# Batch 2's scaled r and k turned by the transposing DMA, with a new stored order and a stored PSUM bank for every tile

## The chip, the cores and the metric

One Trainium2 chip, one of its cores. The metric is the device time of one execution in microseconds (us). A core has five engines with a queue each, and each works through its queue in order: TensorE (PE, matrix products), ScalarE (ACT), VectorE (DVE), GpSimd (POOL) and SyncE (SP), which here only issues DMAs. PE writes to PSUM, which this kernel uses as 8 banks of 128 x 512 fp32; everything else lies in SBUF, 128 partitions wide.

## The reference, cut to what matters

Inputs are r, k, v, w of shape [4, 8, 768, 48] (batch, head, step, channel), u [8, 48], and two weights, 384 x 1536 and 1536 x 384. A recurrence over the steps is followed by a Fourier mix and a small network:

```python
for t in range(S):                       # attention, per batch and head
    cur = outer(u * k[t], v[t])
    y[t] = r[t] @ (state + cur)
    state = w[t][:, None] * state + outer(k[t], v[t])
x = y.transpose(0, 2, 1, 3).reshape(B, S, H * D)          # [4, 768, 384]
mixed = real(fft(fft(x, axis=1), axis=2))
u = x + mixed
un = (u - mean(u)) / sqrt(var(u) + 1e-6)                   # over the 384
out = u + relu(un @ w_ch1) @ w_ch2
```

## The kernel before, in words

The kernel takes each batch in 6 chunks of 128 steps; `n` is the number of a chunk over all four batches, 0 to 23. Batch 0 takes its chunks in pairs (`attention2`), the others one by one (`attention`).

**Attention of a chunk.** ACT takes the logarithm of w. PE sums it over the steps with a triangular matrix (L933, L937), ACT takes the exponentials (L939, L952). DVE and POOL scale r (L971) and k by them; r and k lie in one tile, `rkh`, 128 steps x 2 x 8 heads x 64 in bf16 (a head's 48 channels are padded to 64). Beside that, POOL or DVE multiply r, k and the bonus u (`rk<-in_r,in_k` and `rk<-rk,ub`), DVE sums over a head (`dc`), and the product with v is `vtd`.

The products of r and k (`amat`, L1003) need them with the channels on the partitions, as tile `rkt`. There are two ways:

- For `n < DMA_T`, PE turns them: `tr_r` (L987) and `tr_k` (L993), four 128 x 128 transposes each into a PSUM bank, and then an eviction of 128 x 512 for each, by ACT (L550) or DVE (L551).
- For `n >= DMA_T`, a single transposing DMA, issued by SP (L979), does it from SBUF to SBUF:

```python
if n >= DMA_T:
    op("sp", T_RK, lambda e: e.dma_start_transpose(out=RKT[i4][:, :, :],
                       in_=RKH[i4][:, :, :, :].rearrange("t x h d -> t (x h d)")),
       r=[("RH", i4), ("KH", i4)], w=[("RTB", i4), ("KTB", i4)], sem="rkt%d" % i4, xfer=T_XFER)
```

`DMA_T` is 18: batch 3 alone goes by DMA. Then DVE masks `amat`'s result (`ah`, L1008), PE computes the state (L1029) and the result (L1050, L1053), and DVE adds `vtd` (L1059), which gives x.

**The mix of a batch.** x is folded into its even and odd parts (`xf`, and for batches from `FOLD` on by way of `sd`); PE multiplies by cosines and sines along the steps (L1117) and the channels (L1140). DVE adds x (`uf`, L1142) and takes mean and variance; ACT or DVE subtract the mean (`un`). `un` is turned by PE for batches 0 and 1 (L1163), by a transposing DMA for batches 2 and 3 (L1169).

**The network of a batch**, per half of 384 steps: 12 times three matmuls with W1 (L1187, 128 x 384), relu to `ht` by ACT (L1194) or DVE (L1192), then for each of three blocks of 128 steps 12 matmuls with W2 (L1205), which DVE scales and adds to `uf` (`osb`, L1209), and a write to the output (L1213). The very last block is made in a piece of 256 and one of 128 columns.

**Loads.** r, k, v and w of each chunk are loaded by SP (L579 in pairs, L587 one by one), each kind into 7 buffers in turn. POOL issues the loads of W1 and W2 (L745).

**The order.** Every instruction is first recorded as an operation with a number, what it reads and what it writes. The tables `ORDER["pe"]`, `["act"]`, `["dve"]`, `["pool"]` and `["sp"]` list the numbers in the order in which each engine does them; where an operation may go to more than one engine (`vec`, `evict`), the table in which it stands decides. The waits follow from what is read and written. `schedule` replays the tables against a model of durations, only to give each PSUM tile a bank: the one that is free first in that model. A tile that takes over a bank waits for all operations of the tile before it in that bank.

Of the kernel before, what the change touches and what calls it, by code (L numbers as in the profile page):

```python
# [7 lines left out]
ALU = mybir.AluOpType  # L8
# [14 lines left out]
DMA_T, DMA_U, T_RK, T_UN, T_XFER = 18, 2, 1750, 2000, 1800  # L23
# [10 lines left out]
ORDER = {  # L34
# [24 lines left out]
    "act": (  # L59
# [13 lines left out]
    "dve": (  # L73
# [15 lines left out]
    "pool": (  # L89
# [11 lines left out]
}  # L101


class _Tile:


# [1175 lines left out]
```

## Time and profile before

Three runs took 184.76, 186.2 and 187.23 us: the median is 186.2. The profiled execution:

| | |
|---|---|
| span of the profiled execution (its own time) | 185.4 us |
| PE busy | 176.7 us, 95% |
| weight loads beside it | 126.0 us, 68% |
| DVE busy | 151.6 us, 82% |
| ACT busy | 128.7 us, 69% |
| POOL busy | 106.6 us, 58% |
| DMA, mean over the span | 157 GB/s, 29.01 MB |
| chain that ended last, by engine | PE 74%, DVE 9%, ACT 7%, DMA 6% |

A slice is a fortieth of the span, 4.6 us. Busy PE is time in which matmuls are on their way, not time at its peak. In a chain of waits each row is the work that the next had to wait for; "L1187 x9" is a run of nine matmuls of that line. In a group's row the number behind the comma is the mean duration of one instruction in ns; then comes the idle time ahead of these instructions and what ended it. The names are those of the program's tiles, with the numbers of buffers left out.

### The profile page before, as it was taken

The numbers are of one execution on the slowest core, as the hardware profiler recorded it, in microseconds if no ns is written. First come the engines' busy times: TensorE is split into PE (matmuls) and PEld (weight loads), VectorE is DVE, ScalarE is ACT, GpSimd is POOL, SyncE is SP. The second block draws the span as 40 slices with busy tenths as digits, with TensorE's granted clock in tenths as the row PEclk, the third lists the DMA queues.
The fourth block names the chain that finished last, engine by engine and source line by source line (L and its number), as shares of the span: only waits on it lengthen the run. The fifth ranks groups of instructions, "written<-read, shape, count | busy, mean of one in ns | idle before, by whom it ended". The sixth has DMA issues, their size and how long they took to land.

```text
span 185.4 us, 4736 instructions
## 1 busy us (share of the span) xinstructions
PE 176.7 (95%) x1824; PEld 126.0 (68%) x1824; DVE 151.6 (82%) x360; ACT 128.7 (69%) x303; POOL 106.6 (58%) x128
## 2 busy tenths in 40 slices
PE   5999999997999999999999999999999999999993
PEld 2355676754788768767785777758788666887771
DVE  7979999999499999999999999999897297180043
ACT  5989999996799577899588789726745513627120
POOL 2359999799958826999694659868645000000000
PEclk9999999998799999999999999999999999999999
DMA  6999998999999899899498399692811005412033
GB/s 158 325 301 257 218 194 176 193 194 186 209 211 196 162 196 216 195 224 212 89 213 174 70 234 164 116 183 56 205 46 42 4 0 139 117 42 88 0 127 127
DMA packets 102600, 29.01 MB, mean 157 GB/s; under 512 B 98865, under 2 KB 102066, under 8 KB 102450
## 3 DMA queue, kind: packets, MB, share of 16 engines
q1 hardware_dynamic: 102034, 26.36, 64.8%
q0 software_dynamic: 544, 2.36, 6.7%
q8 instruction: 14, 0.23, 0.5%
q14 instruction: 8, 0.07, 0.1%
HBM read 23.59 MB, written 4.72 MB: 153 GB/s over the span
## 4 chain that ended last, share of the span: by engine, by line
PE 74%; DVE 9%; ACT 7%; DMA 6%; issue 2%; POOL 1%; POOLq 0%; DVEq 0%; ACTq 0%
PE bank L1205 24%; PE bank L1187 24%; DMA w<-in_moe_w_ch_dram 6%; PE bank L1140 5%; PE bank L1117 3%; DVE ah L856 2%; PE bank L1003 2%; PE bank L1226 2%; PE bank L1053 2%; PE bank L1248 2%; ACT rkt L550 1%; PE bank L1050 1%; ACT lb L541 1%; DVE xf L527 1%; PE bank L933 1%
## 5 line engine op out<-in xcount | busy, mean ns | idle before, releaser
L1187 PE MATMUL bank<-unt,w 128*128 128x384 bf16 x288 | 57.5, 335 | 1.0 <-DMA w<-in_moe_w_ch_dram 0.8
L1194 ACT ACTIVATE ht<-bank 128x384 bf16<-128x384 f32 x88 | 39.9, 496 | 24.4 <-PE bank L1187 24.0
L1205 PE MATMUL bank<-w,ht 128*128 128x384 bf16 (+2 forms) x300 | 53.0, 320 | 0.0
L1187 PEld LDWEIGHTS bank<-unt,w 128*128 128x128 bf16 x288 | 38.5, 145 | 8.3 <-DMA w<-in_moe_w_ch_dram 1.0
L1205 PEld LDWEIGHTS bank<-w,ht 128*128 128x128 bf16 x300 | 28.0, 98 | 15.6
L1209 DVE SCALAR_TENSOR_TENSOR osb<-bank,rstd,uf 128x384 f32<-128x384 f32 (+2 forms) x25 | 14.4, 594 | 17.8 <-PE bank L1205 13.3
L1008 DVE TENSOR_TENSOR ah<-bank,msk 128x512 bf16<-128x512 f32 x36 | 23.2, 678 | 0.9 <-PE bank L1003 0.7
L527 POOL TENSOR_TENSOR rkh<-in_k,e 128x384 bf16<-128x384 f32 x20 | 19.9, 997 | 5.6 <-ACT e L952 5.3
L527 POOL TENSOR_TENSOR rk<-rk,ub 128x384 f32<-128x384 f32 x18 | 18.6, 1038 | 5.5 <-DVE rk L527 2.4
L527 POOL TENSOR_TENSOR vtd<-in_v,dc 128x384 f32<-128x384 f32 (+1 forms) x22 | 18.1, 827 | 3.7 <-DVE dc L960 3.7
L527 POOL TENSOR_TENSOR rk<-in_r,in_k 128x384 f32<-128x384 f32 x18 | 18.2, 1020 | 0.0
L541 ACT ACTIVATE un<-uf,agg 128x384 bf16<-128x384 f32 x20 | 12.1, 615 | 7.1 <-DVE agg L1148 7.1
L550 ACT ACTIVATE rkt<-bank 128x512 bf16<-128x512 bf16 x24 | 15.1, 633 | 1.6 <-PE bank L987 1.6
L527 POOL TENSOR_TENSOR sd<-x 128x385 f32<-128x385 f32 x9 | 9.4, 1046 | 11.2 <-DVE sd L527 5.4
L1142 DVE TENSOR_TENSOR uf<-bank,x 128x384 f32<-128x384 f32 x24 | 12.9, 549 | 2.4 <-PE bank L1140 2.2
L527 POOL TENSOR_TENSOR xf<-sd 128x382 bf16<-128x382 f32 (+1 forms) x9 | 10.4, 1164 | 4.5 <-DVE sd L527 4.3
L1146 DVE BATCH_NORM_STATS2 bst<-uf 128x6 f32<-128x384 f32 x24 | 12.7, 546 | 0.1
L939 ACT ACTIVATE bank<-bank 128x384 f32<-128x384 f32 x18 | 8.8, 493 | 5.7 <-PE bank L933 5.7
L1059 DVE TENSOR_TENSOR x<-bank,vtd 128x384 f32<-128x384 f32 x18 | 9.7, 547 | 3.3 <-PE bank L1053 3.3
L541 ACT ACTIVATE lb<-in_w 128x384 bf16<-128x384 f32 (+1 forms) x21 | 12.1, 576 | 0.3 <-PE bank L798 0.2
L541 ACT ACTIVATE vb<-in_v 128x384 bf16<-128x384 f32 x22 | 11.4, 532 | 0.0
L952 ACT ACTIVATE e<-bank 128x392 f32<-128x392 f32 (+1 forms) x18 | 8.9, 497 | 2.5 <-DVE bank L1037 1.1
(167 smaller groups left out, 356.4 us busy)
## 6 DMA issues: line engine op xcount, KB each, us to landing
out_dram<-osb SPq DMA_DIRECT2D x23, 192.0 KB, 2.3
in_w<-in_w_dram SPq DMA_DIRECT2D x18, 192.0 KB, 4.3
in_k<-in_k_dram SPq DMA_DIRECT2D x18, 192.0 KB, 4.0
in_r<-in_r_dram SPq DMA_DIRECT2D x18, 192.0 KB, 3.9
in_v<-in_v_dram SPq DMA_DIRECT2D x18, 192.0 KB, 3.8
w<-in_moe_w_ch_dram POOLq DMA_DIRECT2D x2, 1152.0 KB, 10.6
in_w<-in_w_dram SPq DMA_DIRECT2D x3, 384.0 KB, 4.6
in_k<-in_k_dram SPq DMA_DIRECT2D x3, 384.0 KB, 4.6
```

Source lines behind the costliest of these rows:

```text
L527: return lambda e: e.tensor_tensor(out=o, in0=a, in1=b, op=f)
L541: return lambda e: e.activation(o, a, f, **kw)
L550: {"act": lambda e: e.activation(o(), i(), ACTF.Copy), "dve": lambda e: e.tensor_copy(out=o(), in_=i())}, **kw)
L1008: masked[n] = op("dve", v_1(512), lambda e, x=x: e.tensor_tensor(out=ah[:, x:H:2, :], in0=ps(ta[x])[:, :].rearrange("p (h t) -> p h t", t= ...
L1059: op("dve", v_1(DM), lambda e: e.tensor_tensor(out=xb[:, c, 0:DM], in0=ps(ty)[:, 0:DM], in1=vtd[:, :, :].rearrange("t h d -> t (h d)"), op ...
L1140: return e.matmul(ps(t)[:, 0:DM], (hcs if kb < NP else HCR)[:, j, a:a + 128], DTM[:, j, :], start=(j == 0), stop=(j == 2))
L1142: op("dve", v_1(DM), lambda e, kb=kb, t=t: e.tensor_tensor(out=uf[:, kb, :], in0=ps(t)[:, 0:DM], in1=xb[:, kb, 0:DM], op=ALU.add), r=[t, ( ...
L1146: op("dve", v_1(DM), lambda e, kb=kb, bs=bs: e.bn_stats(bs[:, :], uf[:, kb, :]), r=[("UF", i, kb)], w=[("BST", n % 4)])
L1187: ins = e.matmul(ps(t)[:, 0:384], W1[:, m, j:HID:NJ], unt[:, :, m, :], start=(m == 0), stop=(m == NM - 1))
L1194: "act": lambda e, j=j, t=t, ht=ht: e.activation(ht[:, j, :], ps(t)[:, 0:384], ACTF.Relu, scale=-1.0)},
L1205: ins = e.matmul(ps(t)[:, 0:hi - lo], ht[:, j, 128 * x:128 * x + 128], W2[:, j, lo:hi], start=(j == 0), stop=(j == NJ - 1))
L1209: op("dve", v_1(hi - lo) + 64, lambda e, kb=kb, t=t, o=o, lo=lo, hi=hi: e.scalar_tensor_tensor(out=o[:, lo:hi], in0=ps(t)[:, 0:hi - lo], s ...
```

## The change

`DMA_T` goes from 18 to 12, so that the six chunks of batch 2 (n = 12 to 17) take the transposing DMA too. The 12 groups of four transposes on PE and their 12 evictions go, and six transposing DMAs come onto SP. All five tables in `ORDER` are new. A second table, `BANKS`, has for each bank the tiles that use it in order; `schedule` shrinks to taking the engine from `ORDER` and the bank from `BANKS`, and the waits of an instruction are sorted by its place in the order. The model of durations is gone; the numbers that were its costs remain in the calls and change nothing in the program.

```diff
-DMA_T, DMA_U, T_RK, T_UN, T_XFER = 18, 2, 1750, 2000, 1800
+DMA_T, DMA_U, T_RK, T_UN, T_XFER = 12, 2, 1300, 1300, 1800
...
 ORDER = {
     "pe": (
-        "6 1437 1438 1439 1440 1441 1442 1443 86 92 1444 1445 1446 94 1447 1448 80 1449 1450 97 1451 1452 113 115 "
...
+        "6 1419 1420 1421 1422 1423 1424 86 1425 1426 1427 1428 1429 92 1430 1431 1432 1433 94 1434 80 82 97 1435 1436 "
...
+BANKS = (
+    "0 10 89 97 92 48 98 101 51 60 62 113 55 58 119 79 182 86 135 137 203 152 202 191 205 253 161 206 251 271 234 238 "
+    "282 287 288 302 308 315",
...
-    def schedule(self, order):
+    def schedule(self, order, banks):
         self.order = {e: [self.ops[int(i)] for i in order[e].split()] for e in self.ENGS}
...
         for e in self.ENGS:
             for o in self.order[e]:
                 o.eng = e
-                o.dur, o.fn, o.port = o.alts[e]
...
+                o.fn = o.alts[e][1]
+        for b, line in enumerate(banks):
+            last = None
+            for i in line.split():
+                t = self.tiles[int(i)]
+                t.bank = b
+                if last is not None:
+                    t.ops[0].deps |= set(last.ops)
+                last = t
...
-                for c, v, d in sorted(o.waits, key=lambda x: x[2].end):
+                for c, v, d in sorted(o.waits, key=lambda x: x[2].at):
...
-    g.schedule(ORDER)
+    g.schedule(ORDER, BANKS)
```

The instructions per engine: the changed kernel has 48 matmuls fewer on PE; DVE takes 20 of the relu evictions instead of 8, and 6 evictions of `rkt` instead of 12; ACT takes 76 relu evictions instead of 88, and 18 of `rkt` instead of 24.

Lines in the changed kernel: `tr_r` L908, `tr_k` L914, the transposing DMA of r and k L900, `amat` L924, state L950, `vec` L448, loads L508, the loads of W1 and W2 L666, cosines and sines L1038, W1 L1108, W2 L1126, `osb` L1130, writes L1134.

**SP.** The queue while batch 2's inputs are loaded, before:

```order
43 L587 DMA in_v<-in_v_dram 128x8x48 x3
44 L587 DMA in_w<-in_w_dram 128x8x48 x2
45 L587 DMA in_v<-in_v_dram 128x8x48
46 L587 DMA in_k<-in_k_dram 128x8x48
47 L587 DMA in_r<-in_r_dram 128x8x48 x2
48 L587 DMA in_w<-in_w_dram 128x8x48
49 L1213 DMA out_dram<-osb 128x384 x2
50 L587 DMA in_k<-in_k_dram 128x8x48
```

and now; `rkt<-rkh` is the transposing DMA of a chunk, the first two are those of batch 2's chunks 0 and 1:

```order
41 L508 DMA in_v<-in_v_dram 128x8x48
42 L900 DMA_TRANSPOSE rkt<-rkh 128x8x128
43 L508 DMA in_w<-in_w_dram 128x8x48
44 L900 DMA_TRANSPOSE rkt<-rkh 128x8x128
45 L508 DMA in_k<-in_k_dram 128x8x48
46 L508 DMA in_v<-in_v_dram 128x8x48
47 L508 DMA in_k<-in_k_dram 128x8x48
48 L1134 DMA out_dram<-osb 128x384 x2
49 L508 DMA in_r<-in_r_dram 128x8x48
50 L1134 DMA out_dram<-osb 128x384
51 L508 DMA in_r<-in_r_dram 128x8x48 x2
```

Between the loads of batch 2 now stand transposes, each of which waits for `rkh`.

**POOL.** Its queue up to the load of W1 (`w1<-`), from the same product of v on, before:

```order
21 L527 TENSOR_TENSOR vtd0<-in_v,dc0 128x384
22 L527 TENSOR_TENSOR rk0<-rk0,ub 128x384
23 L527 TENSOR_TENSOR rkh3<-in_k,e2_0 128x8x48
24 L531 TENSOR_SCALAR sd<-sd,th 128x128 x2
25 L527 TENSOR_TENSOR rk2<-in_r,in_k 128x384
...
37 L527 TENSOR_TENSOR xf0<-x0 128x192
38 L527 TENSOR_TENSOR xf0<-x0 128x191
39 L745 DMA w1<-in_moe_w_ch1_dram 128x3x1536
40 L527 TENSOR_TENSOR rk2<-rk2,ub 128x384
```

and now:

```order
29 L448 TENSOR_TENSOR rk1<-rk1,ub 128x384
30 L448 TENSOR_TENSOR rk2<-rk2,ub 128x384
31 L448 TENSOR_TENSOR vtd0<-in_v,dc1 128x384
32 L448 TENSOR_TENSOR xf0<-x0 128x192
33 L448 TENSOR_TENSOR rkh2<-in_k,e2_0 128x8x48
34 L448 TENSOR_TENSOR vtd1<-in_v,dc2 128x384
35 L448 TENSOR_TENSOR xf0<-x0 128x191 x2
36 L448 TENSOR_TENSOR xf0<-x0 128x192
37 L448 TENSOR_TENSOR xf0<-x0 128x191
38 L666 DMA w1<-in_moe_w_ch1_dram 128x3x1536
39 L448 TENSOR_TENSOR xf0<-x0 128x192
40 L448 TENSOR_TENSOR xf0<-x0 128x191
```

Counted over the whole queue ahead of it: before, 2 of the `sd` masks, 2 products of r and k, 3 products with the bonus and 8 folds `xf`; now no `sd` mask, 1 product of r and k, 5 with the bonus and 5 folds. Two folds moved behind it; the fills (memsets) differ by a few small ones.

**PE.** A place in batch 2 where r and k were turned, before:

```order
227 L1117 MATMUL bank<-cs,xf 128x193 x6
228 L993 MATMUL bank<-idw,rkh 128x128 x4
229 L1117 MATMUL bank<-ss,xf 128x193
230 L1117 MATMUL bank<-cs,xf 128x193
231 L1029 MATMUL bank<-vb,rkh 128x96 x4
232 L987 MATMUL bank<-idw,rkh 128x128 x4
233 L1117 MATMUL bank<-cs,xf 128x193 x3
```

and the same stage now:

```order
227 L1038 MATMUL bank<-cs,xf 128x193 x4
228 L1126 MATMUL bank<-w,ht 128x384 x4
229 L924 MATMUL bank<-rkt 128x128 x8
230 L1038 MATMUL bank<-cs,xf 128x193 x4
231 L1038 MATMUL bank<-ss,xf 128x193 x2
```

The transposes (L993, L987) are gone; `amat` (L924) waits for the DMA. At the program's end, PE's last rows before:

```order
519 L1205 MATMUL bank<-w,ht 128x384 x12
520 L1205 MATMUL bank<-w,ht 128x256 x8
521 L1205 MATMUL bank<-w,ht 128x128 x4
522 L1205 MATMUL bank<-w,ht 128x384 x4
523 L1205 MATMUL bank<-w,ht 128x128 x4
524 L1205 MATMUL bank<-w,ht 128x384 x8
```

and now:

```order
462 L1126 MATMUL bank<-w,ht 128x384 x20
463 L1126 MATMUL bank<-w,ht 128x256 x8
464 L1126 MATMUL bank<-w,ht 128x128 x12
```

The narrow pieces of the last block, which stood between those of other blocks, now come last, and DVE's last `osb` is 128 wide instead of 384.

More of the change, by code (lines that the diff above doesn't have):

```diff
@@ L35 @@
     "pe": (
[23 rows of a table removed]
-    "act": (
[13 rows of a table removed]
-    "dve": (
[15 rows of a table removed]
-    "pool": (
[11 rows of a table removed]
-}
[21 rows of a table added]
+    "act": (
[11 rows of a table added]
+    "dve": (
[14 rows of a table added]
+    "pool": (
[11 rows of a table added]
+}
+BANKS = (
[15 rows of a table added]
+)
 class _Tile:
-    __slots__ = ("bank", "ops", "pool", "n_done", "end")
+    __slots__ = ("bank", "ops", "pool")
     def __init__(self, pool):
@@ L112, in __init__ @@
         self.ops = []
-        self.n_done = 0
-        self.end = 0
 class _Op:
@@ L122, in __init__ @@
         self.deps = set()
-        self.users = []
         self.tile = []
         self.sem = None
-        self.nbytes = 0
-        self.start = None
-        self.end = None
         self.inc = False
-        self.ready0 = 0
 class _Prog:
     ENGS = ("pe", "act", "dve", "pool", "sp")
-    TAIL = {"pe": 165, "act": 110, "dve": 85, "pool": 45, "sp": 0}
-    LAT = {"pe": 70, "act": 50, "dve": 45, "pool": 90, "sp": 60}
-    DMA_SET, DMA_POST, DMA_SW = 1400, 300, 2000
-    SWITCH = 95
-    COLD = 7050
     def __init__(self, nc):
@@ L149, in __init__ @@
         self.rd = {}
+        self.tiles = []
     def tile(self, pool):
-        return _Tile(pool)
+        t = _Tile(pool)
+        self.tiles.append(t)
+        return t
     def op(self, eng, dur, fn, r=(), w=(), sem=None, xfer=0, port=(), tiled=False):
@@ L185, in op @@
         return o
-    def schedule(self, order):
+    def schedule(self, order, banks):
         self.order = {e: [self.ops[int(i)] for i in order[e].split()] for e in self.ENGS}
-        at = {e: 0 for e in self.ENGS}
-        engt = {e: 0 for e in self.ENGS}
-        port = {"dve": 0, "pool": 0}
-        bank = [None] * 8
-        sw_t = 0
-        tiled = False
-        hw, sw = [], []
         for e in self.ENGS:
@@ L198, in schedule @@
                 o.eng = e
-                o.dur, o.fn, o.port = o.alts[e]
-        for o in self.ops:
-            for d in o.deps:
-                d.users.append(o)
-            o.nd = len(o.deps)
-            o.r_pe, o.r_other = 0, o.ready0
-            o.opens = [t for t in o.tile if t.ops[0] is o]
-        for left in range(len(self.ops)):
-            best = None
-            for e in self.ENGS:
-                if at[e] == len(self.order[e]):
-                    continue
-                o = self.order[e][at[e]]
-                if o.nd:
-                    continue
-                s = o.r_other if e == "pe" else max(o.r_other, o.r_pe)
-                free = sorted((t.end if t else 0, i) for i, t in enumerate(bank) if t is None or t.n_done == len(t.ops))
-                if len(free) < len(o.opens):
-                    continue
-                if o.opens:
-                    s = max(s, free[len(o.opens) - 1][0])
-                s = max(engt[e], s + self.LAT[e] if s else 0)
-                late = 1
-                if o.port:
-                    p = port["pool" if e == "dve" else "dve"]
-                    late = int(e == "dve" or p <= s)
-                    s = max(s, p)
-                if best is None or (s, late) < best[0]:
-                    best = ((s, late), e, o, free)
-            assert best is not None, "no operation can start"
-            (s, _), e, o, free = best
-            at[e] += 1
-            for t, (_, i) in zip(o.opens, free):
-                t.bank = i
-                if bank[i] is not None:
-                    o.deps |= set(bank[i].ops)
-                bank[i] = t
-            dur = o.dur * 2 if e == "pe" and s < self.COLD else o.dur
-            if e == "pe" and o.tiled != tiled:
-                dur += self.SWITCH
-                tiled = o.tiled
-            engt[e] = s + dur
-            if o.port:
-                port[e] = s + o.dur
-            if o.sem is not None and e == "pool":
-                a = max(sw_t, s + self.DMA_SW)
-                sw_t = a + o.xfer
-                sw.append((a, sw_t))
-                o.end = sw_t + self.DMA_POST
-                t = 0
-                for h in hw:
-                    if h[2].end - self.DMA_POST > a:
-                        h[2].end = self._land(max(t, h[0]), h[1], sw) + self.DMA_POST
-                        for u in h[2].users:
-                            u.r_other = max(u.r_other, h[2].end)
-                    t = h[2].end - self.DMA_POST
-            elif o.sem is not None:
-                t = hw[-1][2].end - self.DMA_POST if hw else 0
-                hw.append((s + self.DMA_SET, o.xfer, o))
-                o.end = self._land(max(t, s + self.DMA_SET), o.xfer, sw) + self.DMA_POST
-            else:
-                o.end = s + dur + self.TAIL[e]
-            o.start = s
-            for t in o.tile:
-                t.n_done += 1
-                t.end = max(t.end, o.end)
-            for u in o.users:
-                if e == "pe":
-                    u.r_pe = max(u.r_pe, o.end)
-                else:
-                    u.r_other = max(u.r_other, o.end)
-                u.nd -= 1
@@ L273, in schedule @@
-        self.total = max(o.end for o in self.ops)
-    @staticmethod
-    def _land(t, dur, sw):
-        for a, b in sw:
-            if t + dur <= a:
-                break
-            if t < b:
-                dur -= max(0, a - t)
-                t = b
-        return t + dur
+                o.fn = o.alts[e][1]
[7 more added lines that the diff above has]
+                last = t
@@ L291, in emit @@
         dcount = {}
-        for o in self._topo():
+        for at, o in enumerate(self._topo()):
+            o.at = at
             kn = known[o.eng]
@@ L541, in act, with vec @@
         return lambda e: e.activation(o, a, f, **kw)
-    def vec(n, fn, **kw):
-        return op(None, {"pool": p_1(n), "dve": v_1(n)}, fn, port=("dve",), **kw)
+    def vec(n, fn, slow=0, **kw):
+        return op(None, {"pool": p_1(n) + slow, "dve": v_1(n)}, fn, port=("dve",), **kw)
     def evict(o, i, n, x=1, more=0, **kw):
@@ L578, in load_two @@
         i = c % NIN
-        o = op("sp", 750, lambda e: e.dma_start(
+        o = op("sp", 450, lambda e: e.dma_start(
             INA[n][:, i:i + 2, :].rearrange("p x (h d) -> p (x h) d", h=H // 2),
@@ L692, in sines @@
         for q in range(NP):
-            step(270, act(put(SS, q), two(TF[q]), ACTF.Sin, scale=sc), r=[("TF", q), "TRIG"],
+            step(398, act(put(SS, q), two(TF[q]), ACTF.Sin, scale=sc), r=[("TF", q), "TRIG"],
                  w=[("SSl", q), "SINS"])
-            step(350, act(put(CS, q), two(TQ[q]), ACTF.Sin, scale=-sc, bias=BHPI[:, :]),
+            step(479, act(put(CS, q), two(TQ[q]), ACTF.Sin, scale=-sc, bias=BHPI[:, :]),
                  r=[("TQ", q), "BHPI", "TRIG"], w=[("CSl", q), "SINS"])
@@ L879, in state @@
             return ins
-        op("pe", mm(96, 8) + 30, state, r=[("KH", y) for y in st4] + vbt, w=tss, tiled=True)
+        op("pe", mm(96, 8) + 10, state, r=[("KH", y) for y in st4] + vbt, w=tss, tiled=True)
         for a in range(2):
@@ L1069, in fold @@
         if b < FOLD:
-            vec(192, tt(xf[:, c, 64:256], xb[:, c, 0:192], xb[:, c, 384:192:-1], ALU.add),
+            vec(192, tt(xf[:, c, 64:256], xb[:, c, 0:192], xb[:, c, 384:192:-1], ALU.add), 50,
                 r=[("X", i, c)], w=[("XFe", i, c)])
-            vec(191, tt(xf[:, c, 256:447], xb[:, c, 1:192], xb[:, c, 383:192:-1], ALU.subtract),
+            vec(191, tt(xf[:, c, 256:447], xb[:, c, 1:192], xb[:, c, 383:192:-1], ALU.subtract), 45,
                 r=[("X", i, c)], w=[("XFo", i, c)])
@@ L1083, in fold @@
         both = [("X", i, p), ("X", i, c)]
-        vec(DM, tt(sd[:, 0, 0:DM + 1], xb[:, p, 0:DM + 1], xb[:, c, 0:DM + 1], ALU.add), r=both, w=[("SD", z, 0)] + HALVES)
-        vec(DM, tt(sd[:, 1, 0:DM + 1], xb[:, p, 0:DM + 1], xb[:, c, 0:DM + 1], ALU.subtract), r=both, w=[("SD", z, 1)] + HALVES)
+        vec(DM, tt(sd[:, 0, 0:DM + 1], xb[:, p, 0:DM + 1], xb[:, c, 0:DM + 1], ALU.add), 40, r=both, w=[("SD", z, 0)] + HALVES)
+        vec(DM, tt(sd[:, 1, 0:DM + 1], xb[:, p, 0:DM + 1], xb[:, c, 0:DM + 1], ALU.subtract), 40, r=both, w=[("SD", z, 1)] + HALVES)
         have = [("SD", z, 0), ("SD", z, 1)]
-        vec(DM, tt(xf[:, p:NC:NP, 64:256], sd[:, :, 0:192], sd[:, :, 384:192:-1], ALU.add),
+        vec(DM, tt(xf[:, p:NC:NP, 64:256], sd[:, :, 0:192], sd[:, :, 384:192:-1], ALU.add), 270,
             r=have, w=[("XFe", i, p), ("XFe", i, c)])
```

8 lines of the change are left out of this document (4 added, 4 removed), and 128 rows, old and new, of tables (BANKS, ORDER).

## The prediction

> **What bounds the kernel now.** I read the page's engine table and slices first, then busy time in the stretch from 50 to 130 us, then the chain of waits at the two places where TensorE is not simply working.
>
> ```profile
> span 185.4 us, 4736 instructions
> ...
> PE 176.7 (95%) x1824; PEld 126.0 (68%) x1824; DVE 151.6 (82%) x360; ACT 128.7 (69%) x303; POOL 106.6 (58%) x128
> ...
> DVE  7979999999499999999999999999897297180043
> ...
> PEclk9999999998799999999999999999999999999999
> DMA  6999998999999899899498399692811005412033
> ```
>
> TensorE (PE) is busy for 95% of the span, at full clock (PEclk) but for two slices. VectorE (DVE) is as full until about 130 us and then has room; ScalarE and GpSimd have room. The next row is the sum of eight windows of 10 us, 50 to 130 us; the two after it are a stage in which PE is short of work, and what follows it (busy us and instructions of PE, weight loads, DVE, ACT, POOL; then the granted clock, the DMA engines' share and GB/s).
>
> ```profile
> sum 80.00, PE 79.31 PEld 59.22 DVE 78.00 ACT 62.84 POOL 60.17; mean PE 9.91 PEld 7.40 DVE 9.75 ACT 7.85 POOL 7.52
> ```
>
> ```profile
> 40.00:44.70 4.70, 3.19 (x41) 1.86 (x38) 4.44 (x13) 4.18 (x10) 4.70 (x7) 1.00 1.11 216
> 44.70:48.00 3.30, 3.25 (x13) 1.94 (x14) 2.11 (x6) 1.37 (x3) 3.30 (x4) 0.53 0.77 152
> ```
>
> From 50 to 130 us PE lacks 0.7 of 80 us, so a matmul removed there is time removed, as long as DVE, with 2.0 us to spare, keeps up. From 40.0 to 44.7 PE works for 3.19 of 4.70 us, and in the 3.30 us after that the granted clock is 0.53. The chain of waits names what ends that stage, and what ends the kernel (start us, us, what).
>
> ```profile
> 33.83 10.87 DMA w<-in_moe_w_ch_dram
> ...
> 44.74 3.05 PE bank L1187 x9
> 47.80 0.43 PE bank L987 x4
> ...
> 65.58 0.22 PE bank L987 x4
> ...
> 158.64 2.92 PE bank L1187 x18
> ...
> 176.17 5.46 PE bank L1205 x44
> ...
> 181.72 0.61 DVE osb L1209
> ...
> 182.37 0.62 DVE osb L1209
> ```
>
> The first W1 matmuls wait for W1's DMA, which GpSimd issues at 33.83 and which lands 10.87 us later. At half clock nine W1 matmuls take 3.05 us, 339 ns each, against 2.92/18 = 162 ns later; four transposes take 0.43 instead of 0.22. So the half clock costs 9 x 0.177 + 0.21 = 1.8 us.
>
> **Part 1: the transposes leave TensorE.** Four transposes cost PE 0.22 us (the row at 65.58). Six chunks of batch 2 with two such groups: 12 x 0.22 = 2.64 us, in the stretch from 65 to about 100 us where PE is full. The evictions that go with them (mean ns behind the comma):
>
> ```profile
> L550 ACT ACTIVATE rkt<-bank 128x512 bf16<-128x512 bf16 x24 | 15.1, 633 | 1.6 <-PE bank L987 1.6
> ...
> L551 DVE COPY rkt<-bank 128x512 bf16<-128x512 bf16 x12 | 5.3, 438 | 0.4 <-PE bank L993 0.3
> ...
> L1192 DVE TENSOR_SCALAR ht<-bank 128x384 bf16<-128x384 f32 x8 | 4.1, 549 | 0.4 <-PE bank L1187 0.4
> ...
> L527 DVE TENSOR_TENSOR rk<-rk,ub 128x384 f32<-128x384 f32 x6 | 4.0, 684 | 0.0
> ```
>
> ACT loses 6 of them (3.8 us), but has room: nothing. DVE loses 6 (2.6 us) and three products with the bonus (3 x 0.684 = 2.1), and gains 12 relu evictions (12 x 0.549 = 6.6); smaller swaps add about 0.2. That is some +2 us on DVE, of which I put half behind 130 us, where slices 29 to 40 read 897297180043 and the room covers it. The other half takes 1 of the 2.0 us to spare; without that cover it would cost up to 2.
>
> **Part 2: six transposing DMAs on SP.** Batch 3 shows them (KB not given, median us to landing; then a window that holds one alone; then of SP's queue three loads, two loads and one transpose, start us and us):
>
> ```profile
> rkt<-rkh SPq DMA_TRANSPOSE x6, 3.4
> ```
>
> ```profile
> 104.70:106.20 1.50, 1.50 (x17) 1.28 (x14) 1.32 (x4) 0.57 (x2) 0.39 (x1) 1.00 0.97 181
> ```
>
> ```profile
> 62.49 2.62 SPq L587 DMA_DIRECT2D in_v<-in_v_dram  x3
> ...
> 69.01 1.74 SPq L587 DMA_DIRECT2D in_r<-in_r_dram  x2
> ...
> 103.42 1.34 SPq L979 DMA_TRANSPOSE rkt<-rkh  x1
> ```
>
> ```profile
> in_r<-in_r_dram SPq DMA_DIRECT2D x18, 192.0 KB, 3.9
> ```
>
> One fills the 16 DMA engines for about 1.5 us and lands after 3.4 us. Six are 9 us of transfer, in a stage where the share is 0.9 to 1.0 (DMA slices 14 to 19, 60 to 88 us, read 899899). The wait that is new: on SP a transpose waits for scaled r and k, and behind it in SP's in-order queue stand loads of batch 2 (two such places are shown with the change). The first pair stands behind v of batch 2's first chunk, the first of the three loads at 62.49, done by about 63.1; PE turned r of that chunk at 65.58. So I estimate that SP reaches the first transpose some 2.5 us before its data. So behind a pair, loads are late by up to 2.5 + 2 x 1.5 = 5.5 us. Their slack: r of two chunks was issued by 70.75, landed by 70.75 + 3.9 = 74.7, and is first read at 77.85 and 78.85:
>
> ```profile
> 77.85 2.00 POOL L527 TENSOR_TENSOR rk<-in_r,in_k 128x384 f32<-128x384 f32 x2
> ```
>
> That is about 4.3 us for the later. So one pair may miss by 1.2 us, which I charge as a wait of DVE and PE: **+1.2** (bounds: 0, if SP gets there later than I think, and rival 2). The Trainium skill, "DMA: Bandwidth & Descriptors", section "Latency and other measured facts", gives transposing DMAs 261 GB/s; by it one of these (128 x 1024 in bf16, 256 KB) would take an estimated 1.0 us instead of 1.5, and the 1.2 us would shrink to 0.2. The row's 181 GB/s decides.
>
> **Part 3: W1 is asked for earlier.** GpSimd is busy right up to W1's issue, so what stands ahead of it counts:
>
> ```profile
> 31.34 2.54 POOL L527 TENSOR_TENSOR xf<-x 128x191 bf16<-128x191 f32 x4
> ```
>
> ```profile
> L527 POOL TENSOR_TENSOR rk<-rk,ub 128x384 f32<-128x384 f32 x18 | 18.6, 1038 | 5.5 <-DVE rk L527 2.4 <-ACT ub L550 2.1 <-ACT e L952 1.1
> L527 POOL TENSOR_TENSOR rk<-in_r,in_k 128x384 f32<-128x384 f32 x18 | 18.2, 1020 | 0.0
> ...
> L527 POOL TENSOR_TENSOR xf<-x 128x192 bf16<-128x192 f32 x4 | 2.7, 680 | 0.5 <-ACT x L550 0.4
> L527 POOL TENSOR_TENSOR xf<-x 128x191 bf16<-128x191 f32 x4 | 2.4, 614 | 0.0
> ...
> L531 POOL TENSOR_SCALAR sd<-sd,th 128x128 bf16<-128x128 f32 x2 | 1.2, 604 | 0.0
> ```
>
> Gone from ahead of it: two masks (1.21), one product of r and k (1.02), three folds (2 x 0.68 + 0.61 = 1.97). New ahead of it: two products with the bonus (2.08) and small fills. Net 2.1 us earlier, 1.5 if the fills and a later first start take some back. PE waited only this long:
>
> ```profile
> 44.74 3.05 PE L1187 MATMUL bank<-unt,w 128*128 128x384 bf16 x9 [0.78 <-DMA w<-in_moe_w_ch_dram]
> ```
>
> So **−0.78**; what is late next is the attention of batch 1, which already holds PE back from 40 us on. With W1 there at some 43 us PE gets dense work inside the stage that now ends in the low clock. I think the drop goes, **−1.8**, but no row shows the limit at which it comes, so it is a rival of its own.
>
> **Part 4: the end.** Before, two 384-wide results of DVE stand behind PE's last matmul, and then a 192 KB write. Now the last piece is 128 wide:
>
> ```profile
> 181.07 0.35 DVE L1209 SCALAR_TENSOR_TENSOR osb<-bank,rstd,uf 128x128 f32<-128x128 f32 x1 [0.50 <-PE bank L1205]
> ```
>
> ```profile
> out_dram<-osb SPq DMA_DIRECT2D x23, 192.0 KB, 2.3
> ...
> out_dram<-osb SPq DMA_DIRECT2D x1, 64.0 KB, 1.5
> ```
>
> ```profile
> L1205 PEld LDWEIGHTS bank<-w,ht 128*128 128x128 bf16 x300 | 28.0, 98 | 15.6
> ```
>
> DVE: 0.35 for 0.61 + 0.62, −0.88. The write: 1.5 for 2.3, −0.8. Against that, twelve 128-wide matmuls in a row run at the pace of their weight loads, 98 ns instead of 0.22/4 = 55: +0.5; and two writes follow closely on SP: I add 0.4. Sum **−0.8** (bounds −0.5 and −1.7).
>
> PE's first dummy matmuls also start a little earlier. They only warm the clock while the first loads arrive, so they count nothing.
>
> Sum: 185.4 − 2.64 + 1.2 − 0.78 − 1.8 − 0.8 = 180.6 us for the profiled span. The profiled execution lies 0.8 under the median of the three runs, 186.2 (184.76 to 187.23), so the forecast is **181.4**.
>
> **Rivals.**
>
> 1. *The half clock stays.* For it: the same stage keeps PE at 3.19 of 4.70 us, and the change moves W1 by 2 us only. Against: W1 fills the last microsecond of it. Time: 181.4 + 1.8 = 183.2, within 2%. The Trainium skill, "TensorE: Matmul & The Clock Gate", section "HAM oscillation — how this bites in real kernels", says to avoid idle gaps of more than about 3.4 us; by that nothing should have dropped here, since the longest gap is 0.78 us, and this case's clock of 0.53 speaks against the rule as it stands. That page's next section, "A second HAM failure mode: psum-queue depth-cycling", on frequent micro-idles between groups of matmuls, fits the row and favours this rival. Chance 0.19.
>
> 2. *The DMA queue takes the place of PE's transposes.* Scaled r and k come from loads that stand behind an earlier transpose on SP, so lateness adds up. Price: three holds of 2.5 and 9 us of transfers make 16.5, less 4.3 of slack once: 12.2, if the DMA engines have nothing to give. Then 181.4 − 1.2 + 12.2 = 192.4, slower. It decides from the point where the loads of batch 2's later chunks land after their first read. With the room that the DMA engines show later (this window of 10 us and the next have shares of 0.63 and 0.75, 6.2 us free) it is 6.0 us and 186.2:
>
> ```profile
> 90.00:100.00 10.00, 9.56 (x89) 7.26 (x87) 10.00 (x20) 7.86 (x19) 6.73 (x7) 1.00 0.63 141
> 100.00:110.00 10.00, 10.00 (x111) 7.63 (x112) 9.70 (x21) 7.70 (x23) 6.66 (x6) 1.00 0.75 147
> ```
>
> For it: the DMA share near 1.0 up to 90 us. Against: batch 3's six ran with PE at 10.00 of 10.00 in the second window. Chance 0.18, 0.11 of it for the dear form.
>
> 3. *DVE becomes the bound.* It is 97.5% busy where PE is relieved, so the 2.64 may not be had, and another 1 us of work may come on top: 181.4 + 2.64 + 1 = 185.0. Chance 0.14.
>
> That batch 2 isn't turned by DMA after all is excluded by the order of instructions.
>
> **How the numbers follow.** Forecast 0.46, rivals 0.19, 0.18 and 0.14, and 0.03 for something worse. About 2%, 3.7 us, is what a measurement of this kernel can tell from no change: under 182.5 is faster, over 189.9 slower. Faster: the forecast and a little of rival 1, 0.48. Slower: the dear form of rival 2 and the rest, 0.14. Within: 0.38. The forecast's own range is 179.3 (no late load, −1.2, and the end at its best, −0.9) to 182.7 (the end at its worst, +0.3, and another 1 us of DVE that is not covered). For 8 in 10 I take 179.0 to 187.0: that includes rivals 1 and 3 and the cheap form of 2.
>
> **What would show it.** Right: no transposes of scaled r and k on PE behind batch 1, PE at 10.00 of 10.00 there, a clock of 1.00 from 44 to 48 us, W1's wait gone, 0.35 us of DVE behind PE's last matmul. Wrong: PE idle before the masked product of r and k (L924 now) or before DVE's x (the name of attention's result) with a DMA named as releaser; load landings of batch 2 more than 4 us later than now, relative to their use; the low clock in the same place or in a new one.

## The result, and the profile after

The changed kernel takes 0.989 of the time before (95% interval 0.984 to 0.994): 1.1% faster, within the 2% that count as no change. A second comparison, on another occasion, gave 0.982 (0.977 to 0.987). The medians of all runs, changed kernel first, are 185.56 us (182.24 to 192.38, 11 runs) and 185.49 us (184.76 to 187.23, 11 runs); on the second occasion 183.07 (180.85 to 191.13, 6 runs) and 184.82 us. The medians of the first are so close because six of the changed kernel's eleven runs took 185.6 to 192.4 us, and the ratio leaves such slow runs out.

The profiled execution of the changed kernel has a span of 180.4 us, and took 182.24 us. From the page:

```profile
span 180.4 us, 4637 instructions
...
PE 171.3 (95%) x1776; PEld 122.9 (68%) x1776; DVE 153.5 (85%) x364; ACT 120.8 (67%) x285; POOL 112.1 (62%) x130
...
PEclk9999999999999999999999999999999999999999
DMA  5999999999999979999969999899970303401323
```

PE has lost 5.4 us of work, and the low clock is gone. Some 2.2 us of the 5.4 are not the change's: a second profile of the kernel before, in the experiments, has 174.5 us of PE and no low clock. DMA is fuller than before, and for longer. The sum of eight windows from 50 to 130 us, and the two windows around the former low clock:

```profile
sum 80.00, PE 79.56 PEld 58.72 DVE 74.37 ACT 58.74 POOL 65.83; mean PE 9.95 PEld 7.34 DVE 9.30 ACT 7.34 POOL 8.23
```

```profile
40.00:44.70 4.70, 4.70 (x59) 3.26 (x56) 4.70 (x16) 4.57 (x10) 4.49 (x6) 1.00 0.96 189
44.70:48.00 3.30, 3.30 (x30) 2.63 (x29) 3.27 (x8) 3.24 (x9) 3.22 (x5) 1.00 1.02 206
```

PE lacks 0.4 of 80 us, with the transposing DMAs of batch 2 in that stretch. DVE has more room there than before, 74.37 for 78.00, though it is busier over the whole span. At the end stands a wait that is new (chain of waits, start us, us, what; the second fence is the chain from 176 us on):

```profile
166.58 0.63 DVE osb L1130
167.20 0.02 issue
167.22 0.33 SPq L1134
167.55 0.04 issue
167.59 4.32 DMA out_dram<-osb
...
172.00 0.63 DVE osb L1130
172.63 0.05 issue
172.68 1.47 PE bank L1126 x8
```

```profile
175.84 2.04 PE bank L1126 x23
177.89 0.02 issue
177.91 0.35 DVE osb L1130
```

DVE waits for a write that is issued at 167.59 and lands 4.32 us later, because it needs the buffer `osb`, of which there are three; PE waits for DVE at 172.68. After PE's last matmul follow only 0.35 us of DVE and the last write: 180.4 − 177.9 = 2.5 us. Before, PE's last matmuls were these (start us, us):

```profile
176.00 6.26 PE L1205 MATMUL bank<-w,ht 128*128 128x384 bf16 x48
```

They end at 182.26, so 185.4 − 182.3 = 3.1 us stood behind them. The chain of waits in the prediction leaves PE at 181.63, 44 matmuls into its row; the four that follow run beside DVE's first result, and only the second result stands behind PE's last matmul.

### The profile page after: what moved, and what is told of

Its sections match the earlier page's. It is cut to its first block, busy times and chain, and to the rows that moved or that the text cites. A ratio compares the mean times of both kernels' runs of the same rounds, so it can differ in the third digit from the quotient of the medians.

```text
span 180.4 us, 4637 instructions
## 1 busy us (share of the span) xinstructions
PE 171.3 (95%) x1776; PEld 122.9 (68%) x1776; DVE 153.5 (85%) x364; ACT 120.8 (67%) x285; POOL 112.1 (62%) x130
## 4 chain that ended last, share of the span: by engine, by line
PE 75%; DVE 11%; DMA 5%; ACT 5%; issue 2%; POOL 1%; SPq 1%; DVEq 0%; POOLq 0%
PE bank L1108 23%; PE bank L1126 21%; PE bank L1061 7%; DMA out_dram<-osb 5%; PE bank L1038 4%; PE bank L924 3%; PE bank L974 2%; PE bank L858 2%; PE bank L854 2%; PE bank L950 1%; PE bank L1084 1%; DVE ah L777 1%; DVE sd L448 1%; DVE osb L1130 1%; PE bank L971 1%
## 5 line engine op out<-in xcount | busy, mean ns | idle before, releaser
L1126 PE MATMUL bank<-w,ht 128*128 128x384 bf16 (+2 forms) x300 | 53.1, 320 | 1.1 <-DVE osb L1130 1.1
L1108 PE MATMUL bank<-unt,w 128*128 128x384 bf16 x288 | 53.5, 329 | 0.1
L1115 ACT ACTIVATE ht<-bank 128x384 bf16<-128x384 f32 x76 | 35.1, 494 | 22.4 <-PE bank L1108 21.9
L1108 PEld LDWEIGHTS bank<-unt,w 128*128 128x128 bf16 x288 | 38.8, 144 | 6.8 <-ACT ht L1115 0.4
L1126 PEld LDWEIGHTS bank<-w,ht 128*128 128x128 bf16 x300 | 27.7, 98 | 17.6 <-DVE osb L1130 1.4
L1130 DVE SCALAR_TENSOR_TENSOR osb<-bank,rstd,uf 128x384 f32<-128x384 f32 (+2 forms) x25 | 14.8, 595 | 11.4 <-DMA out_dram<-osb 6.8
L448 POOL TENSOR_TENSOR rk<-rk,ub 128x384 f32<-128x384 f32 x21 | 21.5, 1032 | 4.3 <-DVE rk L448 3.5
L448 POOL TENSOR_TENSOR rkh<-in_k,e 128x384 bf16<-128x384 f32 x20 | 20.2, 1016 | 1.8 <-ACT e L873 0.8
L448 POOL TENSOR_TENSOR vtd<-in_v,dc 128x384 f32<-128x384 f32 (+1 forms) x21 | 17.6, 844 | 4.0 <-DVE dc L881 3.3
L448 POOL TENSOR_TENSOR rk<-in_r,in_k 128x384 f32<-128x384 f32 x18 | 18.3, 1019 | 0.3 <-DMA in_r<-in_r_dram 0.2
L448 POOL TENSOR_TENSOR xf<-sd 128x384 bf16<-128x384 f32 (+1 forms) x11 | 12.2, 1111 | 7.8 <-DVE sd L448 7.6
L1113 DVE TENSOR_SCALAR ht<-bank 128x384 bf16<-128x384 f32 x20 | 10.8, 552 | 5.1 <-PE bank L1108 5.0
L471 ACT ACTIVATE rkt<-bank 128x512 bf16<-128x512 bf16 x18 | 11.6, 662 | 0.1
L448 POOL TENSOR_TENSOR sd<-x 128x385 f32<-128x385 f32 x8 | 8.8, 1105 | 3.3 <-DVE x L980 2.3
L892 DVE TENSOR_TENSOR rkh<-bank,in_r 128x384 bf16<-128x384 f32 x18 | 9.9, 548 | 0.6 <-ACT bank L860 0.6
```

The source lines that it names most:

```text
L448: return lambda e: e.tensor_tensor(out=o, in0=a, in1=b, op=f)
L471: {"act": lambda e: e.activation(o(), i(), ACTF.Copy), "dve": lambda e: e.tensor_copy(out=o(), in_=i())}, **kw)
L1108: ins = e.matmul(ps(t)[:, 0:384], W1[:, m, j:HID:NJ], unt[:, :, m, :], start=(m == 0), stop=(m == NM - 1))
L1113: {"dve": lambda e, j=j, t=t, ht=ht: e.tensor_scalar(out=ht[:, j, :], in0=ps(t)[:, 0:384], scalar1=-1.0, scalar2=0.0, op0=ALU.mult, op1=AL ...
L1115: "act": lambda e, j=j, t=t, ht=ht: e.activation(ht[:, j, :], ps(t)[:, 0:384], ACTF.Relu, scale=-1.0)},
L1126: ins = e.matmul(ps(t)[:, 0:hi - lo], ht[:, j, 128 * x:128 * x + 128], W2[:, j, lo:hi], start=(j == 0), stop=(j == NJ - 1))
```

## The experiments

In kernels whose tables print on more lines, line numbers are 8 (on the changed kernel's base) or up to 3 (on the kernel before) higher.

**The kernel before, a second look.** No edit.

> The kernel before once more, for a second profiled execution. Its time of 187.2 us (span 185.4) in the profile that the prediction used is 1.7 us over the median of all executions. Theory: the low clock at 45 to 48 us belongs to that execution; here the span is about 183 and the clock 1.00 throughout, with W1's wait still there. Rival: the low clock is usual, span 185.

Measured: span 183.2 us, 184.97 us. Its windows, and PE's row of the first W1 matmuls (start us, us; the bracket is the wait ahead of it):

```profile
40.00:44.70 4.70, 3.77 (x45) 2.40 (x43) 4.44 (x14) 4.03 (x9) 4.70 (x7) 1.00 1.12 219
44.70:48.00 3.30, 3.30 (x31) 2.83 (x30) 2.86 (x8) 3.29 (x8) 3.30 (x5) 1.00 1.01 199
```

```profile
43.97 1.68 PE L1187 MATMUL bank<-unt,w 128*128 128x384 bf16 x9 [0.16 <-DMA w<-in_moe_w_ch_dram]
```

The clock is 1.00 throughout, and PE waits for W1 by 0.16 us instead of 0.78. Nine W1 matmuls take 1.68 us instead of 3.05. The prediction had read both terms from an execution of 187.2 us. That this second profile shows the usual case is borne out by the 56 executions of the kernel before that were taken beside the experiments: six have a mean granted clock under 0.995, and these are the six that took 187.0 us or more. In all 56 the time is 1.75 to 1.87 us over the span (here 184.97 and 183.2), so a span of 185.4 belongs to the longest of the three runs shown, not to one just under their median.

**PE's transposes put back.** The changed kernel's order of all other work, with batch 2's r and k turned by PE:

```diff
-DMA_T = 12
+DMA_T = 18
 # pe: the two groups of four transposes stand 2.8 us (in the changed kernel's trace) ahead of each amat of batch 2
 # act: their two evictions behind them; sp: the six transposing DMAs struck out
```

> The changed kernel's order of all other work, with batch 2's r and k turned by PE again: 48 transposes, their 12 evictions on ACT, six DMA transposes fewer, banks chosen by the model of the kernel before. Theory (the transposes are PE time that is removed): 2.64 us slower than the changed kernel, 1.003 of the kernel before. Rival (the DMA queue is the bound and takes back what PE saves): as the changed kernel or faster, 0.985 to 0.99.

Measured: 0.995 (0.991 to 1.000; all 12 runs 182.91 to 209.46 us), against 0.982 (0.977 to 0.987) for the changed kernel on the same chip at the same time. The difference, 1.3% or 2.5 us, agrees with the 2.64 us of the theory within the two intervals; some 0.35 us of it lie outside the span, since the time is here 2.1 to 2.2 us over it. PE's busy time rises from 171.3 to 173.9 us. So the reordering alone is worth little, and the DMA queue doesn't take the saving back when the order fits it.

**DMA transposes in the old order.** The kernel before, with `DMA_T` at 12 and PE's order otherwise untouched:

```diff
-DMA_T = 18
+DMA_T = 12
 # pe, act, dve: the transposes of batch 2 and their evictions struck out
 # sp: each transposing DMA stands where its data was ready in the trace of before
```

> The kernel before with its own order, but batch 2's r and k turned by DMA: the 12 groups of transposes and their evictions are struck out, and each transposing DMA stands on SP where its data was ready in the trace of before. PE's order is not touched, so the products of r and k stand where they stood. Ready to landing is some 3.4 us; by the trace the products come 6.5, 2.1, 3.7, 2.8, 2.4 and 5.1 us after the data, so PE waits about 1.3 + 0.6 + 1.0 = 2.9 us. Theory: 2.64 saved, 2.9 lost, about as before, 0.995 to 1.005. If the DMA queue were the bound, loads would come late too and it would be slower, over 1.01; if PE's saving held whatever the order, 0.986.

Measured: 1.062 (1.058 to 1.067), far over what any theory had. PE's waits from 60 to 130 us (total, times, longest), and two windows:

```profile
PE bank L1006 <- DMA rkt<-rkh: 8.6, 3, 5.6
PE bank L1006 <- ACT ht L1197: 1.6, 2, 1.0
```

```profile
70.00:80.00 10.00, 4.14 (x37) 2.95 (x38) 4.05 (x8) 2.03 (x5) 4.36 (x6) 0.74 1.26 240
...
90.00:100.00 10.00, 8.27 (x83) 5.61 (x84) 6.34 (x12) 2.64 (x7) 5.49 (x7) 0.83 0.79 164
```

and SP's queue at the longest of them:

```profile
65.61 1.71 SPq L982 DMA_TRANSPOSE rkt<-rkh  x1
67.38 0.61 SPq L590 DMA_DIRECT2D in_w<-in_w_dram  x1
68.03 0.63 SPq L590 DMA_DIRECT2D in_v<-in_v_dram  x1
68.70 1.51 SPq L590 DMA_DIRECT2D in_k<-in_k_dram  x1
70.26 1.71 SPq L590 DMA_DIRECT2D in_r<-in_r_dram  x2
72.01 0.84 SPq L590 DMA_DIRECT2D in_w<-in_w_dram  x1
72.89 1.84 SPq L982 DMA_TRANSPOSE rkt<-rkh  x1
```

The second transpose is issued at 72.89, behind six loads which SP passes on one by one; it lands at 76.8 (3.92 us in the chain of waits), and PE (5.59 us of wait, up to 76.95) has stood before the product since 71.4. Its data was complete at 69.34, with the scaled k:

```profile
68.79 0.55 DVE L530 TENSOR_TENSOR rkh<-in_k,e 128x384 bf16<-128x384 f32 x1
```

So 3.5 of the 5.6 us are the place on SP; the other 2 are PE's order, which has the product at 71.4. 5.6 us of wait is not all: the granted clock is 0.74 in that window and 0.83 in the later one, after a wait of 2.7 us. The expectation had counted 3.4 us from data to landing, without the queue ahead. Loads were not what came late. With this order of PE and these places on SP the DMA is a loss; whether PE's old order would do with the transposes earlier on SP was not tried. In the new order PE does other work until the transpose has landed: there the products start at 71.27 and 73.14 us without a wait, though SP itself stood 2.1 us before the first transpose (its load ended at 63.19, the transpose went at 65.25).

**The output writes.** The changed kernel, with two entries of SP's table moved:

```diff
-"... 1309 1333 1047 1086 1369 1091 1081 1364 ..."
+"... 1309 1333 1047 1091 1081 1086 1369 1364 ..."
```

> The changed kernel, but two output writes of batch 2 that are ready at 153.1 and 156.1 us are issued by SP before the two writes that are ready at 161.9 and 167.2 us, behind which they stand now. Theory: the wait of DVE for a write to land, and PE's idle 1.2 and 0.2 us behind it at 172.7 and 174.2 us, are made by that order alone, so about 1.4 us goes: 0.981 of the kernel before. Rival (the writes are slow because the DMA engines are full, or the time is set elsewhere): no change, 0.989.

Measured: 0.980 (0.974 to 0.985), beside 0.982 for the changed kernel: the gain isn't clear of the noise, but the wait is gone. At the end of the chain the work of PE now runs on:

```profile
177.92 1.95 PE bank L1134 x12
179.87 0.49 PE bank L1116 x3
180.35 4.81 PE bank L1134 x40
```

That execution was a long one, 189.48 us with a span of 187.7, for another reason, which the following rows show: its chain of waits, ACT's waits from 28 to 50 us, GpSimd's row of W1's load, SP's row of the load of w for batch 1's fourth chunk, and a window.

```profile
31.58 10.59 DMA in_w<-in_w_dram
42.17 0.02 issue
42.19 0.52 ACT lb L470
```

```profile
ACT lb L470 <- DMA in_w<-in_w_dram: 5.3, 1, 5.3
```

```profile
31.38 0.99 POOL L674 DMA_DIRECT2D w<-in_moe_w_ch_dram  x1
...
31.58 0.63 SPq L516 DMA_DIRECT2D in_w<-in_w_dram  x1
```

```profile
40.00:50.00 10.00, 6.74 (x41) 4.03 (x41) 3.36 (x9) 6.03 (x13) 5.16 (x6) 0.66 1.01 196
```

W1's load was issued 0.2 us before the load of w, which then took 10.59 us instead of some 3.7. ACT, the attention and PE waited, and the clock fell. In the profile of the changed kernel it is the other way round:

```profile
31.29 0.78 SPq L508 DMA_DIRECT2D in_w<-in_w_dram  x1
...
32.40 0.99 POOL L666 DMA_DIRECT2D w<-in_moe_w_ch_dram  x1
```

Two queues run towards each other here. In four profiles with this order of loads (the changed kernel's two, this one and that of the old banks below) w went out 1.1 and 3.1 us ahead of W1, 0.2 us behind it, and 1.4 us ahead: the gap varies by some 3 us, and only where W1 was first did w come late.

**W1 much earlier in the kernel before.** This makes that order the rule:

```diff
 # pool: the load of W1 stands ahead of four folds
-"... 133 189 244 140 252 ..."
+"... 252 133 189 244 140 ..."
```

> The kernel before, but GpSimd issues the load of W1 four folds earlier, at some 31.3 us instead of 33.8. Theory of the prediction (W1's wait is 0.78 us and an earlier W1 removes it): 0.996. Theory of the transfers: the load of k for batch 1's second chunk, issued at 31.5 and needed at 36.9, now stands behind W1 and lands at some 42: about 4 to 5 us slower, 1.02 to 1.03, in nearly every execution.

Measured: 190.48 us median against 185.49, 5.0 us slower; five of the six executions took 190.1 to 192.3 us, the sixth 185.65. GpSimd's and SP's row, and the chain:

```profile
31.09 1.01 POOL L747 DMA_DIRECT2D w<-in_moe_w_ch_dram  x1
...
31.11 0.67 SPq L589 DMA_DIRECT2D in_w<-in_w_dram  x1
```

```profile
31.11 9.86 DMA in_w<-in_w_dram
40.97 0.02 issue
40.99 0.52 ACT lb L543
```

The theory of the transfers holds in size; the load that decided was that of w, like above, ahead of the load of k that was named. The prediction's rule, that an earlier W1 removes PE's wait, leaves out the price: it buys at most that wait, and costs 5 us here, where W1 overtakes a load that is needed before it has landed.

**W1 three operations later.** On the changed kernel:

```diff
-"... 133 252 244 250 465 ..."
+"... 133 244 250 465 252 ..."
```

> The changed kernel, but GpSimd issues the load of W1 three operations later, 34.8 us instead of 32.4, about where the kernel before has it (33.8). Theory (the W1 term): PE, which starts W1's matmuls at 43.66 us, waits until about 45 us, 1.3 us more, and a low clock behind that adds up to 1.8: 0.996 without the low clock, 1.005 with it. Rival (the time from 40 us on is set by attention, not by W1): 0.989 as the changed kernel.

Measured: 0.995 (0.990 to 0.999), 1.3% or 2.3 us over the changed kernel beside it. W1 was issued at 35.38, since the folds ahead of it waited for ACT, and PE:

```profile
46.78 1.52 PE L1116 MATMUL bank<-unt,w 128*128 128x384 bf16 x8 [2.94 <-DMA w<-in_moe_w_ch_dram]
```

Here W1's time counts in full. The clock stayed at 1.00 behind this wait of 2.94 us, so the low clock is no fixed price of W1's wait.

**W1 two operations later; and w earlier on SP.** Two ways of taking the two apart:

```diff
 # first kernel, pool
-"... 133 252 244 250 465 ..."
+"... 133 244 250 252 465 ..."
 # second kernel, sp: the load of k for batch 1's fifth chunk (542) goes behind that of w (507)
-"... 451 542 541 450 481 423 480 507 509 ..."
+"... 451 541 450 481 423 480 507 542 509 ..."
```

> The changed kernel, but GpSimd issues the load of W1 two operations later, at some 33.6 us instead of 32.4. Theory: W1's transfer holds back every input load that is issued after it or just ahead of it. The load of w for batch 1's fourth chunk is issued at 31.3 us, only 1.1 us ahead of W1; in the profiled execution of the kernel with reordered writes it came 0.2 us behind W1 (31.58 against 31.38), landed after 10.6 us instead of 3.7, and ACT waited 5.3 us. With 2.3 us between them this no longer happens: the long executions (186 us and over) go, the others stay or lose up to 0.5 us because W1 lands about 1.2 us later: 0.982 to 0.985 of the kernel before, median of all about 182. Rival (the long executions come from something else): a third to a half of them stay.

> The changed kernel, but on SP a load of batch 1's fifth chunk (needed at 40 us) goes behind that of w of the fourth (needed at 35.7), which so is issued about 1.5 us earlier, 2.6 ahead of W1. W1 stays. Theory as for the kernel with W1 a little later: no long executions, and here W1 is as early as before: 0.980 to 0.983, median of all about 182. Rival (W1's place isn't what makes them): a third to a half of the executions stay at 186 us and over.

Measured: W1 later, 0.987 (0.982 to 0.992), median 182.62 us (182.01 to 184.00); w earlier, 0.982 (0.976 to 0.988), median 182.62 (180.73 to 184.89). In neither did an execution pass 185 us, in six each. In the first PE waits 1.07 us for W1. That these mends took the long executions away is not shown, though: the kernel with the old banks (next), with W1 and w in their places of the changed kernel, ran beside them and had none in six either, and the kernel with W1 three operations later, where w went out 3.8 us ahead of W1, still had executions of up to 189.07 us. One long execution is traced to the neighbourhood of W1 and w; what makes the others is open.

**The stored banks.** The changed kernel with the old model's choice of banks:

```diff
-    g.schedule(ORDER, BANKS)
+    g.schedule(ORDER)          # the schedule function of the kernel before
```

> The changed kernel's order of work and its DMA transposes, but the bank of each PSUM tile is chosen by the model of the kernel before instead of the stored table (565 of 911 entries differ). Theory (the banks don't matter, since waits are on data): as the changed kernel, 0.982 to 0.989. Rival (the table avoids waits for a bank): slower, 0.99 to 1.0, with PE waiting for evictions of another tile's bank.

Measured: 0.984 (0.979 to 0.990). The table of banks makes no difference that can be measured.

**Both mends, with all writes reordered.** SP's table of the second kernel above, the two writes, and four earlier ones.

> The changed kernel with both mends on SP: w of batch 1's fourth chunk is loaded before W1's transfer begins, and the output writes stand in the order in which they become ready (two of batch 2 ahead of two later ones, as before, and four of batches 1 and 2 between 129 and 155 us). Theory: no long executions, and none of PE's waits behind writes (0.2 us at 140, 0.6 at 142, 1.4 at 172 to 174 us of the changed kernel's profile): about 2 us below the changed kernel's usual 0.982 to 0.987, 0.972 to 0.977. Rival (the time set by writes is taken back by PE's other waits): 0.982.

Measured: 0.985 (0.980 to 0.989): the rival's 0.982 lies in the interval, the theory's 0.972 to 0.977 doesn't. Two new waits stand against the gain (chain from 30 to 50 us, then PE's waits from 130 to 150 us):

```profile
29.46 2.16 POOL xf L456 x4
31.62 9.70 DMA in_k<-in_k_dram
41.39 1.00 POOL rkh L456
```

```profile
PE bank L1116 <- DMA unt<-un: 1.4, 1, 1.4
```

The load that took w's place met W1 itself (W1 at 31.60), and at 136.8 us PE waited for the transposing DMA of `un`, ahead of which two writes now stood on SP.

**The last one.** w before k on SP, W1 one operation later, and only the two writes of the end:

```diff
 # pool
-"... 133 252 244 250 ..."
+"... 133 244 252 250 ..."
 # sp: 542 behind 507; 1091 and 1081 ahead of 1086
```

> The changed kernel with the load of w before that of batch 1's fifth chunk on SP, the load of W1 one operation later on GpSimd (0.6 us), and only the two output writes of the end reordered. In the kernel with all writes reordered, the load that took w's place was itself caught: issued at 31.62, W1 at 31.60, landed after 9.7 us, PE waited 1.5 us for it at 42.4. Theory: with 0.6 us more between the two no load that is needed before 43 us stands within reach of W1, and PE waits for W1 by 0.3 us at most: 0.975 to 0.980, no execution over 185. Rival: PE's wait for W1 costs as much as the load gains, 0.985.

Measured: 0.979 (0.974 to 0.984), median 181.72 us (181.16 to 184.16) against 185.46. PE waits 0.50 us for W1. Its median is 3.7 us under that of the kernel before taken beside it, the largest such gap of all versions; against the changed kernel (0.982 and 0.989) the gain is not clear of the intervals.

## Why the prediction was right or wrong

The time lies in the range (179.0 to 187.0) and by the ratio the kernel is faster, as forecast; the size was off, 1 to 2% instead of the 2.6% of 181.4 against 186.2, so that it came out within 2%, to which the prediction had given 0.38. That the forecast's span of 180.6 us nearly meets the 180.4 of the profile is partly luck: a late load (+1.2) that didn't come stands in the sum, and a wait for writes (1.1) that came doesn't. Point by point:

- **"12 x 0.22 = 2.64 us"** was right. PE's busy time goes down, PE has no wait from 60 to 105 us, and putting the transposes back costs 2.5 us.
- **"The profiled execution lies 0.8 under the median"** was wrong: a span was set beside times. The time is 1.8 us longer than the span, so that execution was 1.0 over the median of the runs shown. The forecast's 180.6 us of span should have read 182.4 us.
- **"−0.78" and "−1.8" for W1** failed, though the rows were read rightly, and W1 did go out 1.4 us earlier (32.40 for 33.83): the changed kernel's profile has neither wait nor low clock, but that of the second look has only 0.16 us of the one and nothing of the other. Nearly all of the 2.6 us were credited for an event of one execution. Worse, the step did not ask what W1's transfer would overtake when it starts earlier. That made the one long execution that was traced, and the kernel with W1 still earlier lost 5 us by it.
- **Rival 1**, the low clock that stays, can't be judged by the one profile. Over the executions it came oftener: a mean clock under 0.995 in 8 of the changed kernel's 17 and in 6 of 56 of the kernel before; on the second occasion alone 3 of 6 and 3 of 23.
- **"+1.2" for late loads behind the transposes on SP** failed. SP did stand before the first transpose, 2.1 us for the 2.5 estimated, but PE has no wait for it; the transposes were placed so that other work covers them.
- **Rival 2**, the DMA queue in the place of PE's transposes, did not come in the changed kernel. With the old order it did, and dearer: 6% slower. The mechanism was a different one, though: the transpose stood behind loads on SP (3.5 us of the longest wait), not the loads behind the transpose.
- **"DVE, +2 us, half of it in the full stretch"** had the total right (151.6 to 153.5 us) and the place wrong: from 50 to 130 us DVE has 3.6 us less to do. Rival 3 did not come.
- **"−0.8" at the end** was right in kind: 3.1 us behind PE's last matmul became 2.5, so −0.6. The terms were off: −0.88 for DVE took two results to stand behind that matmul, where one does, and from DVE's last result to the end the profiles have 2.1 us for 2.4, −0.3, where −0.8 was reckoned for the write; the +0.5 and +0.4 set against them made up for it. It left out what the same change of order cost ahead of it: two writes that were ready at 153 and 156 us stand on SP behind two that are ready at 162 and 167, and PE waits 1.1 us through DVE and the three buffers. The prediction had moved loads past waits on SP in its mind, and not writes.

Against the second look the span goes from 183.2 to 180.4 us. PE's busy time falls by 3.2 us (174.5 to 171.3), of which 2.64 are the transposes; the rest isn't explained. PE's idle time (us, each stretch less PE's busy time in it) grows by 0.4, and moves:

| stretch | before, second look | changed kernel |
|---|---|---|
| up to 40 us | 3.4 | 4.6 |
| 40 to 50 us | 0.9 | 0 |
| 50 to 130 us | 1.2 | 0.4 |
| 130 us to PE's last matmul | 0 | 1.6 |
| behind it | 3.1 | 2.5 |

What the new order wins from 40 to 130 us and at the end it loses ahead of 40 us, which no experiment takes apart, and behind 130 us, where the wait for writes is 1.1 of the 1.6.

What stays open: what makes most of the changed kernel's long executions, and why the clock fell after a wait of 0.78 us in the first profile of the kernel before and not after 2.94 us in the kernel with a late W1. No run separates the length of the wait from the work around it.

## What to carry to other kernels

Before a wait in a profile is priced, look whether that execution is a usual one: compare its time (not its span) with the others. A big transfer that is started earlier can hold up a load that is issued just behind it; here two queues issue them independently, the gap between them varied by some 3 us from one execution to another, and the load came late by 6 us. Where work moves from an engine to a DMA, look at both orders: when the issuing queue reaches the transfer after its data is ready, and what the waiting engine can do until it lands. On an in-order issuing queue the writes count as much as the loads.

## What the runs showed of the hardware that was not expected

- A load of 192 KB issued 0.2 us after the 1152 KB load of W1 (10.6 us) took 10.59 us, one issued 0.02 us after it (11.0 us) 9.86 us, against a median of 3.9 to 4.5 us for its kind in three profiles: the small load landed only about when the big one did. How the two share the DMA engines is not shown. In the changed kernel's profile a load issued 1.1 us ahead of W1 was not held up (3.7 us); the next of its kind, 1.7 us behind W1, took 10.3 us, and nothing waited for it.
- The granted clock fell to 0.66 (40 to 50 us in the kernel with reordered writes) and 0.74 (70 to 80 us with the old order) after waits of PE of 4.9 and 5.6 us, and stayed at 1.00 after one of 2.94 us. The Trainium skill, "TensorE: Matmul & The Clock Gate", section "HAM oscillation — how this bites in real kernels", puts the limit for idle gaps at about 3.4 us; these three agree. The drop to 0.53 behind 0.78 us in the first profile, and the one to 0.83 (90 to 100 us) behind 2.7 us with the old order, do not.
